# Turning an attention tile's weights two steps behind its scores instead of one

## The chip, the core and the metric

One core of a Trainium2 chip runs the whole program. The metric is the device time of one execution in microseconds; lower is better. Five engines work side by side, each in the order of its own queue: TensorE (PE; its weight loads are shown apart as PEld), VectorE (DVE), ScalarE (ACT), GpSimdE (POOL), and SyncE (SP), which here issues most DMAs. [...]

## The reference

Clustered attention on 2 batches of 8 heads (768 positions, 64 wide), then two mixture-of-experts layers on the 1536 rows of 512 that it gives. The part that matters here:

```python
q_assign = np.argmax(np.einsum('bhsd,hcd->bhsc', q_n, c_n), axis=-1)
k_assign = np.argmax(np.einsum('bhsd,hcd->bhsc', k_n, c_n), axis=-1)
mask = q_assign[:, :, :, None] == k_assign[:, :, None, :]
scores = scale * np.matmul(q, k.transpose(0, 1, 3, 2))
scores = np.where(mask, scores, -1000000000.0)
scores = scores - np.max(scores, axis=-1, keepdims=True)
attn = np.exp(scores)
attn = attn / (np.sum(attn, axis=-1, keepdims=True) + 1e-09)
return np.matmul(attn, v).astype(np.float32)
```

After it come `_moe_ref` (top 2 of 8 experts, noisy logits) and `_moe2_ref` (one expert for each row, with a capacity), each with weights of 512x1024 and 1024x512 for each expert.

## The kernel before

The attention goes through 16 heads of 6 tiles (128 queries by 768 keys): 96 steps `g`, and `LAG` more in which the pipeline runs empty. Float32 values are split into a high and a low part so that products run in a fast format. A step has four slots `s`, and its work is emitted in this order, which is each engine's order:

- Slots 0 and 1: `scores` for one half of the keys, two matmuls each (L678, L679), into the PSUM pool `pst` of two tiles. After slot 1, `top` takes the row maximum on VectorE (L684).
- Slots 2 and 3: `turned_part` turns one half of the tile before: three transposes (L703) into the PSUM pool `pet` (tiles named `et`, three buffers), a copy to `Eh` on ScalarE (L706), the remainder to `El` on VectorE (L707), which frees the `et` buffer.
- In each slot `go_av`: the matmuls of weights with values (`av`, L719 and L721) of a half of a head that is already turned, 12 for every 12 slots, spread as `AV` says (none in two slots, two in the last two). With the last of them ScalarE copies the result to `oT` (L724).
- In each slot `go`: what `PLAN` puts in this slot of the 24 of a head. CL0 to CL3 are the cluster products of the next head (L643) and start a chain of small VectorE steps, one for each later slot; QB, KA, QC and KB are transposes of q and k (L626), each into an `et` buffer with one copy on ScalarE (L629, L631, L633); XB is `xback` of the head before, which multiplies `oT` (L734) and scales (L730 to L742), adds to the logits on GpSimdE (L744) and, after odd heads, stores `xp` (L747); QS, KS and VS split q, k and v on GpSimdE.
- After slot 3, `weights`: the exponential of this step's tile (L692) on ScalarE, into the SBUF tile `E`, of which there are two.

From head 8 on the routing of the first batch (`route1`) runs in small pieces beside this, and in heads 12 to 15 the first experts' weights are split (`wneed0`; L180 on ScalarE, L182 on VectorE or GpSimdE). At the start of the last head `open_first` closes the pool `init`, which lies on the right side of SBUF, and opens the pools of the first expert there; the rows of that expert are turned in steps 2 and 4 of that head (L956, also `et` buffers). After the last step the pools of the attention are closed, and `ring3` with two more pairs of weight tiles lies where they were. The two expert layers follow, with no instruction in them that the change touches.

Of the kernel before, what the change touches and what calls it, by code (L numbers as in the profile page):

```python
# [8 lines left out]
F32 = mybir.dt.float32  # L9
F32R = mybir.dt.float32r  # L10
# [12 lines left out]
def kernel(  # L23
# [19 lines left out]
    C = centroids.shape[1]  # L43
    J = S // 128
    NBH = B * H
    HW = S // 2
    T, Dm = out.shape
    E, _, F = moe_w1.shape
    NT = T // 128
# [8 lines left out]
    NSP = 2  # L58
    NJ1 = E + 2
    GT = 3  # L60
# [7 lines left out]
    Z0, Z1, Z2 = (3, 0.5), (3, 0.5), (3, 2)  # L68
    NC1 = E * R1
    NC2 = (E + NSP) * CT2  # L70
    assert (B, H, S, D, C, E) == (2, 8, 768, 64, 16, 8) and cap % 128 == 0 and cap == 384

# [13 lines left out]
    consts = attn_ctx.enter_context(tc.tile_pool(name="aconst", bufs=1))  # L86
    init_ctx = ExitStack()
    init = init_ctx.enter_context(tc.tile_pool(name="init", bufs=1, side="right"))
# [10 lines left out]
    lane = glob.tile([128, 128], BF16, name="lane")  # L99
    first8 = glob.tile([128, E], F32, name="first8")  # L100
    eoff1 = glob.tile([128, E], F32, name="eoff1")
# [85 lines left out]
    def wfill():  # L187
        while clock["out"] < st.get("ahead", SB) and chunks and not st.get("rush"):
            clock["out"] += 1
            chunks.pop(0)()  # L190
# [16 lines left out]
    def advance(queue=tasks):  # L207
        for g in list(queue):
            try:
                next(g)  # L210
            except StopIteration:
                queue.remove(g)
# [299 lines left out]
    wk = attn_ctx.enter_context(tc.tile_pool(name="awork", bufs=2))  # L512
# [1 line left out]
    pet = attn_ctx.enter_context(tc.tile_pool(name="pet", bufs=3, space=PSUM))  # L514
    pav = attn_ctx.enter_context(tc.tile_pool(name="pav", bufs=1, space=PSUM))

    QTs = [consts.tile([128, J, 128 + C], F32R, name=f"qt{n}") for n in range(2)]
    KTs = [consts.tile([128, J, 192 + C], F32R, name=f"kt{n}") for n in range(2)]
    Vs = [consts.tile([128, J, 2, D], F32R, name=f"vt{n}") for n in range(2)]

    def load(i):
# [11 lines left out]
    def loadv(i):  # L533
        b, h = divmod(i, H)
        st["vraw", i] = io.tile([128, J, D], F32, name="vraw")
        nc.sync.dma_start(st["vraw", i], v[b, h].rearrange("(p j) d -> p j d", j=J))
# [134 lines left out]
    def scores(i, j, half):  # L671

        if half == 0:
            st["S", i, j] = pst.tile([128, 2, 512], F32, name="st")
        ps = st["S", i, j][:, half, :HW]
        js = slice(j * 128, (j + 1) * 128)
        cs = slice(half * HW, (half + 1) * HW)
        nc.tensor.matmul(ps, st["QC", i][:64 + C, js], st["KB", i][:64 + C, cs], start=True, stop=False)  # L678
        nc.tensor.matmul(ps, st["QB", i][:, js], st["KA", i][:, cs], start=False, stop=True)  # L679

    def top(i, j):
        ps = st["S", i, j][:, :, :HW]
        nm = wk.tile([128, 1], F32, name="nm", bufs=3)
        nc.vector.tensor_reduce(nm, ps, axis=AX.XY, op=OP.max, negate=True)  # L684
        st["nm", i, j] = nm

    def weights(i, j):

        if j == 0:
            st["Z", i] = wk.tile([128, J], F32, name="Z", bufs=3)  # L690
        E = wk.tile([128, 2, HW], F32, name="E", bufs=2)
        nc.scalar.activation(E, st.pop(("S", i, j))[:, :, :HW], AF.Exp, bias=st.pop(("nm", i, j)), accum_out=st["Z", i][:, j:j + 1])  # L692
        st["E", i, j] = E

    def turned_part(i, j, part):
        h, jj = divmod(j, 3)
        if jj == 0 and part == 0:
            st["W", i, h] = [wk.tile([128, J, HW], F32R, name=n) for n in ("Eh", "El")]
        Eh, El = st["W", i, h]
        E = st["E", i, j]  # L700
        ps = pet.tile([128, 512], F32, name="et")
        for n in range(3):
            nc.tensor.transpose(ps[:, n * 128:(n + 1) * 128], E[:, part, n * 128:(n + 1) * 128], ident)  # L703
        ps = ps[:, :HW].rearrange("p (n s) -> p n s", n=3)
        o = (slice(None), slice(3 * part, 3 * part + 3), slice(jj * 128, (jj + 1) * 128))
        nc.scalar.activation(Eh[o], ps, AF.Copy)  # L706
        nc.vector.tensor_sub(El[o], ps, Eh[o].bitcast(F32))  # L707
        if part:
            del st["E", i, j]

    def av(i, half, m):
        if m == 0:
            st["acc"] = pav.tile([128, 512], F32, name="acc")
        acc = st["acc"]
        Eh, El = st["W", i, half]
        t, low = divmod(m, 2)
        vt = Vs[i % 2][:, t]
        if low:
            nc.tensor.matmul(acc[:64, :HW], vt[:, 0], El[:, t], start=False, stop=(t == J - 1), skip_group_check=True)  # L719
        else:  # L720
            nc.tensor.matmul(acc[:, :HW], vt.rearrange("p a d -> p (a d)"), Eh[:, t], start=(t == 0), stop=(t == J - 1),  # L721
                             skip_group_check=True)
        if m == 2 * J - 1:
            nc.scalar.activation(oT[:, half * HW:(half + 1) * HW], acc[:, :HW], AF.Copy)  # L724
            del st["acc"], st["W", i, half]

    def xback(i):
# [17 lines left out]
        if h % 2 == 1:  # L745
# [2 lines left out]
                              [:, :, p * 128:(p + 1) * 128], xp.rearrange("p j a d -> p j (a d)"))  # L748


    LAG = 4
    RS = (1, 3, 5, 7, 9, 11, 13, 15, 17, 19, 21, 23)
    WS = {12: 10, 13: 10, 14: 22, 15: 0}
    AV = (0, 0, 1, 1, 1, 1, 1, 1, 1, 1, 2, 2)
    PLAN = {"CL0": 0, "CL1": 0, "CL2": 1, "CL3": 1, "QB0": 4, "QB1": 5, "KA0": 8, "KA1": 9, "QC0": 12, "KB0": 13,
            "XB": 17, "KB1": 16, "QC1": 20, "QS": 0, "KS": 2, "VS": 17}

    def plan(i):

        d = [[] for _ in range(24)]  # L760

        def put(name, fn, *args):
            d[PLAN[name]].append(lambda: fn(*args))

        if i + 1 < NBH:
            for n in range(4):
                put(f"CL{n}", cluster, i + 1, n)
            for n in range(2):
                put(f"QC{n}", trans, i + 1, "QC", n)
                put(f"KB{n}", trans, i + 1, "KB", n)  # L770
        if i + 2 < NBH:
            put("QS", splitq, i + 2)
            put("KS", splitk, i + 2)
            for n in range(2):
                put(f"QB{n}", trans, i + 2, "QB", n)
                put(f"KA{n}", trans, i + 2, "KA", n)
        if 1 <= i < NBH:
            put("XB", xback, i - 1)
        if i < NBH - 1:
            put("VS", vsplit, i + 1)  # L780
        return d
# [490 lines left out]
    def open_first():  # L1272
        init_ctx.close()
        P["first"] = (N2, pool("first", "ex", "right"), pool("first", "eh", "right"))
        st["pairs"] = True
        early_gather()
        st["preps"] = jobs[0].preps()
        st["first"] = jobs[0].hidden()

    for g in range(NBH * J + LAG):  # L1280
        i, t = divmod(g, J)
        if t == 0:
            steps = plan(i)
        if t == 2 and 1 <= i < NBH - 1:
            loadv(i + 1)
        if (i, t) == (3, 5):
            nc.sync.dma_start(out.rearrange("(p n) d -> p n d", n=NT),
                              xgs[0][:, None, :Dm].to_broadcast([128, NT, Dm]))
        if (i, t) == (5, 5):
            nc.sync.dma_start(y_dram.rearrange("(t p c) d -> p t c d", p=128, c=2)[:, :, 1],  # L1290
                              xgs[0][:, None, :Dm].to_broadcast([128, NT, Dm]))
        if (i, t) == (NBH - 6, 0):
            wfill()
        if i == H:
            steps[23] = steps[23] + [lambda: rtasks.append(route1(0, rpsum))] if t == 0 else steps[23]
        if (i, t) == (NBH - 1, 0):
            open_first()
        if (i, t) in PREP:
            st["preps"][PREP[i, t]]()
        if t == 0 and i in WS:  # L1300
            steps[WS[i]].append(wneed0)

        def go(s):
            for step in steps[s]:
                step()
            advance()
            if s in RS:
                advance(rtasks)

        def go_av(s):  # L1310

            w, k = divmod(4 * g + s - 16, 12)
            if 0 <= w < 2 * NBH:
                for m in range(sum(AV[:k]), sum(AV[:k + 1])):
                    av(*divmod(w, 2), m)

        ip, tp_ = divmod(g - 1, J)
        for s in range(4):
            if s < 2 and i < NBH:
                scores(i, t, s)  # L1320
                if s:
                    top(i, t)
            if s >= 2 and 0 <= ip < NBH:
                turned_part(ip, tp_, s - 2)
            go_av(s)
            go(4 * t + s)
            if s == 3 and i < NBH:
                weights(i, t)
# [278 lines left out]
```

## Time and profile before

| | us |
|---|---|
| median of 3 runs | 915.18 (913.13 to 916.36) |
| profiled execution | 916.56 |
| its span | 914.4 |
| TensorE busy, of the span | 855.0 |
| VectorE busy | 563.5 |
| ScalarE busy | 514.5 |
| GpSimdE busy | 225.8 |

The attention takes the first 320 us of the span. All times in the rows below are microseconds from the start of the span. A matmul's end is modelled and overlaps its successor's start, so the distance from start to start says what one costs.

### The profile page before, as it was taken

What the parts mean: (1) busy time and instruction counts of PE and PEld (TensorE: products, weight loads), DVE (VectorE), ACT (ScalarE), POOL (GpSimd) and SP (SyncE); (2) the same over time, 40 slices, a digit from 0 to 9 for tenths busy, and PEclk for the clock granted to TensorE, in tenths of its full rate; (3) what the DMA queues carried; (4) which work ended last, traced back from release to release, by engine and by line L of the source; (5) the groups of instructions that cost most, each with busy time, mean ns of one, the idle gap of its engine ahead of it and who ended that gap; (6) DMA issues with size and microseconds to landing.
All of it is one profiled execution on the core that took longest, in us unless ns stands there. A gap on an engine that the chain in (4) does not pass through costs nothing. (4 is left out here: it accounts for less than half of the span.)

```text
span 914.4 us, 14652 instructions
## 1 busy us (share of the span) xinstructions
PE 855.0 (94%) x5338; PEld 759.2 (83%) x5338; DVE 563.5 (62%) x1174; ACT 514.5 (56%) x977; POOL 225.8 (25%) x273
## 2 busy tenths in 40 slices
PE   5999999999999788899999999999998989999997
PEld 5899899888888677798897988888897768888886
DVE  5888888789898675544733535335375627655271
ACT  4888888888778632443433444336254427655361
POOL 4224223322222043023021230214223412222120
PEclk9999999999999999999999999999899989999999
DMA  3105331231111104555453454446464518776250
GB/s 78 43 27 190 105 121 44 73 116 44 51 50 39 51 18 154 164 177 166 150 190 127 129 162 150 139 155 213 152 227 159 189 34 270 253 231 196 76 175 16
DMA packets 61516, 116.73 MB, mean 128 GB/s; under 512 B 13065, under 2 KB 25097, under 8 KB 61424
## 3 DMA queue, kind: packets, MB, share of 16 engines
q1 hardware_dynamic: 52544, 92.50, 31.4%
q0 software_dynamic: 8880, 23.06, 7.5%
q8 instruction: 51, 0.84, 0.4%
q14 instruction: 41, 0.34, 0.1%
HBM read 97.24 MB, written 23.68 MB: 132 GB/s over the span
## 5 line engine op out<-in xcount | busy, mean ns | idle before, releaser
L182 DVE TENSOR_TENSOR wl<-raw,wh 128x1024 fp32r<-128x1024 f32 x120 | 145.3, 1222 | 41.1 <-ACT wh L180 37.0
L977 PE MATMUL l<-xh,wh 128*128 128x256 f32 (+1 forms) x508 | 157.6, 313 | 8.4 <-DVE hl L980 3.4
L977 PE MATMUL l<-xh,wl 128*128 128x256 f32 (+1 forms) x508 | 156.4, 310 | 0.2 <-DVE wl L182 0.2
L977 PE MATMUL l<-xl,wh 128*128 128x256 f32 (+1 forms) x508 | 150.2, 311 | 0.0
L1022 PE MATMUL l<-wh,hh 128*128 128x512 f32 x328 | 136.6, 416 | 0.8 <-PEq L1194 0.2
L180 ACT ACTIVATE wh<-raw 128x1024 fp32r<-128x1024 f32 x128 | 132.9, 1054 | 5.0 <-DMA raw<-in_moe_w_dram 4.9
L1024 PE MATMUL l<-wh,hl 128*128 128x512 f32 x328 | 131.3, 400 | 0.3 <-DVE hl L994 0.3
L1023 PE MATMUL l<-wl,hh 128*128 128x512 f32 x328 | 130.5, 398 | 0.0
L980 DVE SCALAR_TENSOR_TENSOR hl<-l,hh 128x256 fp32r<-128x256 f32 (+1 forms) x127 | 61.5, 484 | 103.6 <-ACT hh L979 101.5
L979 ACT ACTIVATE hh<-l 128x256 fp32r<-128x256 f32 (+1 forms) x127 | 54.9, 433 | 114.4 <-PE l L977 112.2
L707 DVE TENSOR_TENSOR El<-et,Eh 128x384 fp32r<-128x384 f32 x192 | 103.3, 554 | 21.2 <-ACT Eh L706 18.7
L703 PE MATMUL et<-ident,E 128*128 128x128 f32 x576 | 98.8, 282 | 15.2 <-ACT E L692 12.6
L706 ACT ACTIVATE Eh<-et 128x384 fp32r<-128x384 f32 x192 | 93.8, 491 | 27.3 <-PE et L703 24.7
L977 PEld LDWEIGHTS l<-xh,wh 128*128 128x128 f32 x508 | 96.9, 191 | 12.1 <-DVE hl L980 3.6
L684 DVE TENSOR_REDUCE nm<-st 128x1 f32<-128x768 f32 x96 | 91.6, 954 | 18.8 <-PE st L679 17.7
L977 PEld LDWEIGHTS l<-xh,wl 128*128 128x128 f32 x508 | 96.9, 191 | 1.2 <-DVE wl L182 0.4
L977 PEld LDWEIGHTS l<-xl,wh 128*128 128x128 f32 x508 | 95.3, 191 | 0.4
L703 PEld LDWEIGHTS et<-ident,E 128*128 128x128 f32 x576 | 68.4, 143 | 29.5 <-ACT E L692 23.2
L692 ACT ACTIVATE E<-st,nm 128x768 f32<-128x768 f32 x96 | 86.3, 899 | 2.7 <-DVE nm L684 2.7
L721 PE MATMUL acc<-Eh,vt 128*128 128x384 f32 x192 | 75.5, 393 | 0.6 <-ACT oT L724 0.6
L1024 PEld LDWEIGHTS l<-wh,hl 128*128 128x128 f32 x328 | 62.7, 191 | 15.5 <-DVE hl L994 0.8
L678 PE MATMUL st<-KB,QC 80*128 80x384 f32 x192 | 73.4, 383 | 0.1
(312 smaller groups left out, 1466.2 us busy)
## 6 DMA issues: line engine op xcount, KB each, us to landing
raw<-in_moe_w_dram SPq DMA_DIRECT2D x128, 512.0 KB, 4.4
vraw<-in_v_dram SPq DMA_DIRECT2D x16, 192.0 KB, 2.5
x_dram<-xp SPq DMA_DIRECT2D x8, 384.0 KB, 3.0
out_dram<-xg SPq DMA_DIRECT2D x1, 3072.0 KB, 12.1
y_dram<-xg SPq DMA_DIRECT2D x1, 3072.0 KB, 11.7
part<-y_dram SPq DMA_DIRECT2D x12, 256.0 KB, 4.1
yt<-y_dram SPq DMA_DIRECT2D x12, 256.0 KB, 4.6
x_dram<-part POOLq DMA_DIRECT2D x12, 256.0 KB, 3.9
```

Source lines behind the costliest of these rows:

```text
L180: nc.scalar.activation(wh[:, cs], raw[0], AF.Copy)
L182: eng.tensor_tensor(wl[:, cs], raw[0], wh[:, cs].bitcast(F32), op=OP.subtract)
L684: nc.vector.tensor_reduce(nm, ps, axis=AX.XY, op=OP.max, negate=True)
L692: nc.scalar.activation(E, st.pop(("S", i, j))[:, :, :HW], AF.Exp, bias=st.pop(("nm", i, j)), accum_out=st["Z", i][:, j:j + 1])
L703: nc.tensor.transpose(ps[:, n * 128:(n + 1) * 128], E[:, part, n * 128:(n + 1) * 128], ident)
L706: nc.scalar.activation(Eh[o], ps, AF.Copy)
L707: nc.vector.tensor_sub(El[o], ps, Eh[o].bitcast(F32))
L721: nc.tensor.matmul(acc[:, :HW], vt.rearrange("p a d -> p (a d)"), Eh[:, t], start=(t == 0), stop=(t == J - 1), skip_group_check=True)
L977: nc.tensor.matmul(ps[:, :n], (w1l if k == 2 else w1h)[:, c, fs], (self.xl if k == 1 else self.xh)[:, c, :n], start=(m == 0), stop=(m == l ...
L1022: nc.tensor.matmul(ps[:rows], hh[:, f, cs], w2h[:, f, :], start=(f == 0), stop=False)
L1023: nc.tensor.matmul(ps[:rows], hh[:, f, cs], w2l[:, f, :], start=False, stop=False)
L1024: nc.tensor.matmul(ps[:rows], hl[:, f, cs], w2h[:, f, :], start=False, stop=(f == FC - 1))
```

## The change

The transposes of a tile, and the value matmuls behind them, move one step back; the tile `E` gets a third buffer; the pipeline runs one step longer at its end; three entries of the plan move (XB from slot 17 to 21, QC1 from 20 to 17, VS from 17 to 20); and the split tiles of q and k (17 KB of each partition) move from the pool `aconst`, which lives as long as the attention, to `init`.

```diff
-    QTs = [consts.tile([128, J, 128 + C], F32R, name=f"qt{n}") for n in range(2)]
-    KTs = [consts.tile([128, J, 192 + C], F32R, name=f"kt{n}") for n in range(2)]
+    QTs = [init.tile([128, J, 128 + C], F32R, name=f"qt{n}") for n in range(2)]
+    KTs = [init.tile([128, J, 192 + C], F32R, name=f"kt{n}") for n in range(2)]
...
-        E = wk.tile([128, 2, HW], F32, name="E", bufs=2)
+        E = wk.tile([128, 2, HW], F32, name="E", bufs=3)
...
-    LAG = 4
+    LAG = 5
...
-            "XB": 17, "KB1": 16, "QC1": 20, "QS": 0, "KS": 2, "VS": 17}
+            "XB": 21, "KB1": 16, "QC1": 17, "QS": 0, "KS": 2, "VS": 20}
...
-            w, k = divmod(4 * g + s - 16, 12)
+            w, k = divmod(4 * g + s - 20, 12)
...
-        ip, tp_ = divmod(g - 1, J)
+        ip, tp_ = divmod(g - 2, J)
```

## Rows read from the trace of the kernel before

**Rows 1.** Busy time by engine, heads 1 to 8: from:to length, busy (instructions), clock, DMA.

```profile
36.00:183.00 147.00, 143.85 (x1092) 133.00 (x1091) 121.40 (x242) 126.13 (x290) 43.90 (x66) 1.00 0.28 92
```

**Rows 2.** Waits of TensorE, whole span: who for whom, us in total, times, longest.

```profile
PE et L703 <- ACT E L692: 12.6, 22, 2.0
```

**Rows 3.** The same wait from 36 to 183, 183 to 297, 297 to 320 us.

```profile
PE et L703 <- ACT E L692: 2.4, 8, 0.3
...
PE et L703 <- ACT E L692: 5.2, 8, 2.0
...
PE et L703 <- ACT E L692: 4.2, 4, 1.9
```

**Rows 4.** Time line, head 7's second step: start, us, instruction, [idle before]; last, head 8's first exponential.

```profile
145.85 0.91 ACT L692 ACTIVATE E<-st,nm 128x768 f32<-128x768 f32 x1
...
146.73 0.88 ACT L631 ACTIVATE QB<-et 128x384 fp32r<-128x384 f32 x2
...
146.90 0.55 PE L703 MATMUL et<-ident,E 128*128 128x128 f32 x3 [0.29 <-ACT E L692]
...
147.46 0.49 PE L703 MATMUL et<-ident,E 128*128 128x128 f32 x3
...
163.52 0.91 ACT L692 ACTIVATE E<-st,nm 128x768 f32<-128x768 f32 x1
```

**Rows 5.** Time line from the last value matmul of a half to xback.

```profile
153.24 0.34 PE L719 MATMUL acc<-El,vt 128*64 128x384 f32 x1
...
153.65 0.49 ACT L724 ACTIVATE oT<-acc 128x384 f32<-128x384 f32 x1
...
153.78 0.35 PE L626 MATMUL et<-identr,kt 128*80 128x128 f32 x3
...
154.19 1.48 PEld L734 LDWEIGHTS et<-RW,oT 128*128 128x128 f32 x12
```

**Rows 6.** Time line of the longest wait, head 9.

```profile
182.43 1.28 ACT L692 ACT_TABLE_LOAD   x1
...
184.62 0.86 ACT L631 ACTIVATE QB<-et 128x384 fp32r<-128x384 f32 x2
...
184.77 0.55 PE L703 MATMUL et<-ident,E 128*128 128x128 f32 x3 [2.02 <-ACT E L692]
```

**Rows 7.** Busy time by engine behind it; the granted clock is third from the end.

```profile
185.00:190.00 5.00, 5.00 (x29) 4.62 (x28) 2.96 (x9) 3.62 (x10) 0.00 (x0) 0.66 0.69 272
```

**Rows 8.** Time line, start of the last head: TensorE, VectorE, ScalarE.

```profile
296.28 0.55 PE L703 MATMUL et<-ident,E 128*128 128x128 f32 x3 [1.03 <-ACT E L692]
...
298.35 0.95 DVE L684 TENSOR_REDUCE nm<-st 128x1 f32<-128x768 f32 x1
299.21 1.01 DVE L707 TENSOR_TENSOR El<-et,Eh 128x384 fp32r<-128x384 f32 x2
299.39 0.90 ACT L692 ACTIVATE E<-st,nm 128x768 f32<-128x768 f32 x1 [0.98 <-DVE nm L684]
...
300.43 0.55 PE L703 MATMUL et<-ident,E 128*128 128x128 f32 x3 [1.87 <-ACT E L692]
```

**Rows 9.** Time line, the last tile's maximum and its transposes.

```profile
313.17 0.95 DVE L684 TENSOR_REDUCE nm<-st 128x1 f32<-128x768 f32 x1
...
315.25 0.55 PE L703 MATMUL et<-ident,E 128*128 128x128 f32 x3 [1.24 <-ACT E L692]
```

**Rows 10.** Time line, q's split on GpSimdE and the first transposes that read it.

```profile
159.24 1.02 POOL L574 TENSOR_TENSOR qt<-qraw,qt 128x384 fp32r<-128x384 f32 x1
...
163.28 0.37 PE L626 MATMUL et<-identr,qt 128*128 128x128 f32 x3
```

**Rows 11.** Time line behind the attention: the last store of xp, the second weight buffer's low half.

```profile
323.11 0.53 SPq L747 DMA_DIRECT2D x_dram<-xp  x1
...
327.19 4.86 POOL L182 TENSOR_TENSOR wl<-raw,wh 128x1024 fp32r<-128x1024 f32 x2 [3.40 <-ACT wh L180]
```

**Rows 12.** The page's DMA issues: stores of xp, KB each, median us to landing.

```profile
x_dram<-xp SPq DMA_DIRECT2D x8, 384.0 KB, 3.0
```

## What the change will do to the time

> **What bounds the kernel now.** I read the busy time by stage first. From 36 to 183 us, heads 1 to 8 of the attention, TensorE is busy 143.85 of 147.00 us at full granted clock, its weight loads 133.00, ScalarE 126.13 and VectorE 121.40 [rows 1]. The change touches nothing after the attention, so what it can win is TensorE's idle time inside the attention, and an end of the attention that comes earlier moves everything behind it by as much.
>
> Second I read TensorE's waits. The wait that the change aims at, the transposes at L703 for the exponentials at L692, is 12.6 us in 22 places [rows 2]. By stretch [rows 3]: 2.4 us in heads 1 to 8 (eight waits of 0.3, one for each head), 5.2 from 183 to 297 us (eight waits, one of 2.0), 4.2 in the last head (four); the 0.8 left over lie in the first head. So 12.6 us is the ceiling, 1.4% of the run, and two thirds of it lie in six single places.
>
> Third I read the time line around one wait of each kind, to see what else stands ready to stop TensorE there.
>
> **The new order.** Behind scores(t) TensorE now turns tile t-2, whose exponential ended a step ago. The weight-times-value matmuls follow at the same distance as before, so they stand one step (four slots) later too, and so does all that hangs on them: V's split (slot 17 to 20), the output product xback (17 to 21); QC1 goes from 20 to 17. TensorE's instructions are the same in number and kind. At the start tile 0 is turned one step later and at the end tile 95 is, one tile's six transposes and some value matmuls: work moved, not added. I take 0 for the start (0.8 us of waits there, bounds -0.8 to +0.8), since ScalarE's copies fill the first steps as much as TensorE's work.
>
> **Heads 1 to 8, the wait removed.** The eight waits of 0.29 go: the transposes that started at 146.90 could have at 146.61 [rows 4].
>
> **Heads 1 to 8, what is late next.** Two things. First, ScalarE's order is unchanged: exponential at 145.85, then the two QB copies from 146.73 [rows 4], 0.88 for both, so the first ends at about 147.2. The PSUM pool `et` has three buffers, and a step of four takes QB0, QB1 and the two halves of the turned tile: the second half takes QB0's buffer. It stands behind the exponential by that road, and the third E buffer doesn't touch it. Started with the first half at 146.61 and the value matmul between them (0.56 from half to half, 146.90 to 147.46), it would be ready at 147.17 and may go at about 147.27: a wait of 0.10, in the step with KA0 and KA1, which now has the two value matmuls. Bounds 0 and 0.29 (the whole wait over again).
>
> Second, xback loses its cover. Today the last value matmul of a half starts at 153.24, ScalarE copies it to oT from 153.65 to 154.14, and meanwhile TensorE does four score matmuls and KB1's three transposes; xback's first weight load, which reads oT, stands at 154.19 with no idle ahead of it [rows 5]. In the new plan KB1 (slot 16) lies ahead of the last value matmul (now slot 19), and between it and xback in slot 21 there are the four score matmuls alone. KB1 took from 153.78 to 153.96 and some 0.05 of the next start, so the load would be ready at about 153.95: a wait of 0.24. Bounds: 0, and 0.73 if the copy to oT also comes one more ScalarE copy later (0.49, the oT row), since KB1's and QC1's copies now lie in the same step ahead of it. I take 0.24: the step before xback now (two transposes, six value matmuls) has the make-up of today's (QC0, KB0, six), whose oT is ready as the row says.
>
> Sum of a head: -0.29 + 0.10 + 0.24 = +0.05; for eight +0.4. Bounds -2.4 (nothing late next) and 8 x (-0.29 + 0.10 + 0.73) = +4.3.
>
> [...]
>
> **Heads 9 to 14.** Six waits of 0.2 to 0.8 (5.2 less 2.0, and 1.0 that belongs to the end) make 2.2 us; the two new waits cost 6 x 0.34 = 2.0. Sum -0.2, bounds -2.2 and +2.8 (0.83 a head).
>
> **Head 9, 2.02 us.** At 182.43 ScalarE loads the exponential's table (1.28 us), and the exponential and QB's copies follow; TensorE stands until 184.77 [rows 6]. Now the first half of the turned tile can go at once, but the second needs QB0's copy, which ends at about 185.1, against 185.33 when it started before: 0.2 won, and some 0.15 more because oT's copy is no longer ahead of that exponential. I take -0.35, bounds 0 and -2.0. The granted clock of the five us after this stall was 0.66 [rows 7], a stretch at the lower of the two levels that cost about 0.34 x 5 = 1.7 us of work. Whether it comes again I can't read; 0, bounds -1.7 and +1.7 (one more such stretch).
>
> [...]
>
> **Head 15 and the end.** 1.03 and 1.87 us [rows 8] come from a chain on VectorE and ScalarE: a weight split holds the maximum back until 298.35, the exponential until 299.39. The change frees the turned tile from that exponential but the chain stays, and El, which frees an `et` buffer, is queued behind that maximum (from 299.21, the first ends at about 299.8). So the second half of the tile before could go at about 299.8 instead of 300.43, with the first half (0.3) done already: 0.9 of the 2.9 won. The other three (4.2 + 1.0 - 2.9, so 2.4 us) include 1.24 at 315.25, where the last tile's maximum at 313.17 stands behind xback's four VectorE operations and two El [rows 9]; the plan puts xback behind that maximum now. I take 0.7 of the 2.4, since El and the prepared rows of the first expert (in the same three buffers) are late next. Sum -1.6, bounds 0 and -5.3.
>
> **Edits at no cost.** V's split in GpSimdE's queue now precedes the sum into the logits and, as before, q's split: that split ended at 160.26 and is read at 163.28 [rows 10]; one and a half us of shift leave as much as cover. SyncE's store of xp moves one step and holds nothing that is due. With q's and k's tiles on the right, the later weight tiles lie over other attention tiles: the low half of the second weight buffer, by the sizes, over xp, whose store is issued at 323.11 and lands 3.0 us later at about 326.6, 0.5 us ahead of its first writer, on GpSimdE at 327.19 [rows 11, 12]. If that cover went, GpSimdE's writes would be late by as much; both move together.
>
> **The sum.** 0 + 0.4 - 0.2 - 0.35 - 1.6 = -1.75, about -1.7. The profiled execution took 916.56 us (span 914.4); this gives 914.9. It stood 1.4 above the median, 915.18, so the forecast for a median is 913.5.
>
> **Rivals.**
> 1. *Faster: nothing is late next.* For it: oT's copy and QB0's miss by only 0.2 and 0.1. Heads 1 to 14 give -2.4 - 2.2, head 9 -0.6, the end between -1.6 and -5.3: -6.8 to -10.5, so 905 to 908; with half of the new waits, about 911. Against it: the copy to oT can't start before its last matmul ends.
> 2. *Slower: ScalarE becomes the bound ahead of xback.* In the new plan four steps in a row hold two copies each. If the copy to oT is held by ScalarE's queue and not by its last matmul, it comes up to 0.49 later and xback waits 0.73: heads 1 to 8 +4.3, heads 9 to 14 +2.8, less 0.35 and 1.6, +5.1: 920.3. It decides from the point where ScalarE is idle nowhere between exponential and oT; for it, ScalarE's 126.13 of 147.00; against it, its idle in the steps of xback and of the clusters, where it catches up.
> 3. *It does what it says in name only:* each wait for L692 comes back as one for the copies behind it, to the full. 915.2.
>
> [...]
>
> **How the numbers follow.** A measurement of this kernel can tell about 0.3%, 2.75 us, from no change. Forecast 0.38, its own range 911.5 to 916.5; rival 3 0.08; rival 1 in whole or in half 0.36; rival 2, or a second stretch at the lower clock, 0.18. Forecast and rival 3 lie within 0.3%: 0.46. Faster 0.36, slower 0.18. Leaving out a tenth on either side gives 908.5 to 918.
>
> **What would show it.** Right: L703's waits for L692 under 2 us, new waits at L734 for L724 (about 0.2, once for each head), waits of L703 for copies, heads of 17.6 to 17.8 us (today 17.67, from 145.85 to 163.52 [rows 4]), the last head shorter by 1 to 2 us. Wrong: heads under 17.4 (rival 1), L734 waiting 0.5 or more (rival 2), a low clock somewhere new, or GpSimdE waiting at the second weight buffer.

## The result, and the profile after

The changed kernel takes 903.93 us, median of 4 runs (903.64 to 905.71); the kernel before, run beside it, 914.8 (913.13 to 916.36). The ratio is 0.9883, 95% interval 0.9858 to 0.9909: faster by 10.9 us. The forecast was 913.5, with a range down to 908.5: the sign of the gain was the forecast's, its size was not, and the time lies below the range. The profiled execution took 903.99.

First the page of the kernel after, part 1: the span, TensorE's busy time and its weight loads'.

```profile
span 902.2 us, 14571 instructions
PE 851.7 (94%) x5338; PEld 759.5 (84%) x5338; DVE 559.9 (62%) x1174; ACT 511.6 (57%) x977; POOL 224.5 (25%) x273
```

Next the place of the gain. I cut the span at the first score matmul, at the exponentials of the first tile of heads 1, 8 and 15, at the last value matmul and at the end. Busy time by engine in these five stretches: from:to length, busy (instructions) of PE, PEld, DVE, ACT, POOL, granted clock, share of the DMAs, GB/s. The kernel before:

```profile
17.96:39.79 21.83, 20.96 (x130) 18.93 (x130) 15.72 (x31) 15.79 (x37) 10.43 (x16) 1.00 0.15 43
39.79:163.52 123.73, 121.67 (x927) 112.76 (x925) 103.26 (x204) 106.38 (x246) 37.00 (x55) 1.00 0.28 93
163.52:299.39 135.87, 125.25 (x925) 112.87 (x923) 118.35 (x288) 112.04 (x250) 33.31 (x47) 0.99 0.21 65
299.39:319.46 20.07, 16.06 (x108) 13.89 (x109) 13.61 (x25) 13.25 (x28) 0.39 (x1) 1.00 0.10 32
...
319.46:914.40 594.94, 562.81 (x3206) 493.39 (x3204) 301.88 (x587) 257.66 (x399) 138.90 (x135) 0.98 0.48 157
```

The kernel after, the same cuts:

```profile
17.52:37.08 19.56, 19.26 (x115) 17.22 (x116) 14.04 (x27) 14.24 (x34) 10.43 (x16) 1.00 0.16 52
37.08:158.05 120.97, 120.96 (x926) 112.98 (x925) 101.70 (x204) 104.58 (x247) 36.90 (x55) 1.00 0.28 94
158.05:292.82 134.77, 125.39 (x934) 114.48 (x932) 118.69 (x290) 111.47 (x251) 32.97 (x48) 0.99 0.21 65
292.82:311.49 18.67, 16.52 (x112) 14.62 (x113) 14.35 (x27) 13.96 (x31) 0.39 (x1) 1.00 0.11 39
...
311.49:902.20 590.71, 561.26 (x3206) 492.80 (x3204) 300.58 (x587) 258.04 (x399) 138.12 (x135) 0.98 0.48 158
```

The attention went from 301.50 to 293.97 us (319.46 - 17.96, 311.49 - 17.52), so it gives 7.5: 2.3 in the first stretch, 2.8 in heads 1 to 7 (0.39 a head), 1.1 in heads 8 to 14, 1.4 in the last. The stage behind it, in which no instruction differs, is 4.2 shorter in these two profiles; the experiments come back to that. In heads 1 to 7 the stretch lost 2.76. The matmuls' idle time explains less of it, 2.05 (2.06 to 0.01); the weight loads' fell from 10.97 (123.73 - 112.76) to 7.99, by 3.0.

### The profile page after: what moved, and what is told of

Its sections match the earlier page's. It is cut to its first block, busy times and chain, and to the rows that moved or that the text cites. A ratio compares the mean times of both kernels' runs of the same rounds, so it can differ in the third digit from the quotient of the medians.

```text
span 902.2 us, 14571 instructions
## 1 busy us (share of the span) xinstructions
PE 851.7 (94%) x5338; PEld 759.5 (84%) x5338; DVE 559.9 (62%) x1174; ACT 511.6 (57%) x977; POOL 224.5 (25%) x273
## 5 line engine op out<-in xcount | busy, mean ns | idle before, releaser
L706 ACT ACTIVATE Eh<-et 128x384 fp32r<-128x384 f32 x192 | 91.2, 493 | 19.9 <-PE et L703 17.7
L684 DVE TENSOR_REDUCE nm<-st 128x1 f32<-128x768 f32 x96 | 91.4, 952 | 16.2 <-PE st L679 13.6
L1022 PEld LDWEIGHTS l<-wh,hh 128*128 128x128 f32 x328 | 63.0, 192 | 12.7 <-issue 1.0
```

What stands on the lines that cost most here:

```text
L1022: nc.tensor.matmul(ps[:rows], hh[:, f, cs], w2h[:, f, :], start=(f == 0), stop=False)
```

## The experiments

Medians; "before" is the kernel before, run beside it on the same chip. "Heads" is the mean length of heads 1 to 7, from exponential to exponential of the first tiles, "attention" and "behind" are the two stages as above, in the profiled execution.

| kernel | us | before | ratio (95%) | heads | attention | behind |
|---|---|---|---|---|---|---|
| before | | | | 17.68 | 301.5 | 594.9 |
| the change | 903.93 | 914.8 | 0.9883 (0.9858 to 0.9909) | 17.28 | 294.0 | 590.7 |
| the change again | 906.1 | 921.24 | 0.9858 (0.9817 to 0.9899) | 17.26 | 293.7 | 592.8 |
| memory alone | 915.91 | 914.29 | 1.0008 (0.9979 to 1.0037) | 17.68 | 302.9 | 596.2 |
| plan alone | 917.19 | 914.29 | 1.0042 (1.0017 to 1.0068) | 18.01 | 306.2 | 589.1 |
| order without memory | 905.72 | 914.29 | 0.9920 (0.9889 to 0.9952) | 17.27 | 294.3 | 593.8 |
| other order in xback | 902.0 | 914.29 | 0.9878 (0.9844 to 0.9913) | 17.44 | 294.7 | 591.5 |
| KA1 two slots later | 906.57 | 921.24 | 0.9860 (0.9824 to 0.9895) | 17.26 | 293.3 | 590.9 |
| QC1 back in slot 20 | 908.23 | 921.24 | 0.9873 (0.9840 to 0.9907) | 17.30 | 293.6 | 594.0 |
| KA1 and KB0 later | 910.9 | 921.24 | 0.9905 (0.9870 to 0.9940) | 17.28 | 295.7 | 592.4 |
| weight split later | 904.12 | 912.84 | 0.9898 (0.9857 to 0.9940) | 17.28 | 293.5 | 589.7 |
| xback in slot 20 | 901.63 | 912.84 | 0.9878 (0.9828 to 0.9928) | 17.33 | 293.8 | 587.4 |

Theory after the result: the gain is in the order of TensorE's work, the wait for the exponential was larger than the matmul rows said, and the wait that was forecast ahead of xback isn't there. Rivals: the third buffer or the new memory layout makes the gain; the plan makes it.

**Memory alone.** The kernel before, with the third `E` buffer and q's and k's tiles in `init`:

```diff
-    QTs = [consts.tile( ...
+    QTs = [init.tile( ...
-    KTs = [consts.tile( ...
+    KTs = [init.tile( ...
-        E = wk.tile([128, 2, HW], F32, name="E", bufs=2)
+        E = wk.tile([128, 2, HW], F32, name="E", bufs=3)
```

> The kernel before with the memory edits alone: q's and k's split tiles in the pool closed early, and three E tiles; the order of the work is as before. Theory (the gain comes from the order of the work): 915, within 1.5 us of before, with the weight loads of L703 still waiting about 23 us for L692. Rival (a part of the gain, the 4 us that the changed kernel won after 340 us, comes from where the tiles lie): 910 to 912, and the stage behind the attention shorter by 4.

Ratio 1.0008, heads as before. Waits of the weight loads, 36 to 183 us:

```profile
PEld et L703 <- ACT E L692: 6.3, 16, 0.4
```

They are those of the kernel before (6.4 in 16, below): neither a buffer nor the layout was short. The attention's 1.4 us more go with the granted clock: summed over 5 us windows, (1 - clock) x 5 is 3.4 in it, 1.7 in the kernel before. The gap repeats in each head (16 waits in eight heads) and the third buffer alone gave nothing; the row named the true cause, an exponential still running (0.91 us from 145.85, the transposes behind it at 146.90 [rows 4]).

**Plan alone.** The kernel before, with the three entries moved:

```diff
-            "XB": 17, "KB1": 16, "QC1": 20, "QS": 0, "KS": 2, "VS": 17}
+            "XB": 21, "KB1": 16, "QC1": 17, "QS": 0, "KS": 2, "VS": 20}
```

> The kernel before with the three entries of the plan alone (xback in slot 21, QC1 in 17, V's split in 20), the transposes one step behind as before. Theory (the distance of the transposes wins, not the plan): within 3 us of 915, heads 1 to 8 at 17.5 to 17.9 us. Rival (the plan evens out ScalarE's copies and is most of the gain): heads 1 to 8 at about 17.3 us and 908 or less.

Heads of 18.01, above the 17.5 to 17.9 expected: with the old distance the plan costs 0.33 a head. Its waits, 36 to 183 us, of the weight loads and of the matmuls:

```profile
PEld et L703 <- ACT E L692: 7.7, 16, 0.5
...
PE et L703 <- ACT E L692: 5.3, 16, 0.4
```

From here to the change the only step in the heads is the distance (the third buffer did nothing above). The weight loads' wait of 0.96 a head (7.7 / 8) goes, 0.25 comes (2.0 / 8, the wait for KA shown below), which makes -0.71; the matmuls' wait of 0.66 a head (5.3 / 8) goes and none comes. The heads went from 18.01 to 17.28, -0.73. In this step both measures are near what was won.

**Order without memory.** The change with two `E` buffers and q's and k's tiles back in `aconst`:

```diff
-    QTs = [init.tile( ...
+    QTs = [consts.tile( ...
-    KTs = [init.tile( ...
+    KTs = [consts.tile( ...
-        E = wk.tile([128, 2, HW], F32, name="E", bufs=3)
+        E = wk.tile([128, 2, HW], F32, name="E", bufs=2)
```

> The changed kernel with both memory edits undone: two E tiles, q's and k's split tiles where they were; the order of the work is that of the change. An exponential that writes a tile's E stands on ScalarE behind the copy of the transposes that read it last, so two tiles should do. Theory: 904, within 1.5 us of the changed kernel. Rival (the third buffer or the placement is needed): 907 to 912, with L692 waiting for L703, or the stage after 340 us as long as before.

Busy time by engine of the attention and of the stage behind it:

```profile
17.60:311.92 294.32, 282.49 (x2083) 260.01 (x2084) 248.80 (x545) 243.50 (x559) 80.64 (x119) 0.99 0.23 74
311.92:905.70 593.78, 563.82 (x3206) 494.89 (x3204) 300.35 (x587) 257.56 (x399) 139.27 (x135) 0.97 0.48 157
```

The attention is as short as the change's, 294.3. Two buffers do: the exponential that writes the buffer anew stands on ScalarE behind the copies to `Eh` of the transposes that read it last. In the change such a pair of copies starts at 142.51 and 143.15, and the exponential behind them at 143.91.

**Other order in xback.** The change, with the products that need the copy just made put first:

```diff
-        for j in range(J):
+        for j in (3, 4, 5, 0, 1, 2):
```

> The changed kernel with xback's six products in the order 3, 4, 5, 0, 1, 2, so that the first one reads the half of oT that was copied last. It tests the wait that my prediction priced at 0.24 us for each head and that the changed kernel does not show. Theory (the wait is not there because the first three products read the half copied long before): 0.2 to 0.3 us a head at L734, 15 heads, 907 to 909. Rival (oT comes early enough in any order): 904, no waits at L734.

The time line around xback, the change first (start, us, engine line instruction):

```profile
151.06 0.34 PE L719 MATMUL acc<-El,vt 128*64 128x384 f32 x1
...
151.47 0.48 ACT L724 ACTIVATE oT<-acc 128x384 f32<-128x384 f32 x1
...
151.77 0.81 PEld L734 LDWEIGHTS et<-RW,oT 128*128 128x128 f32 x6
```

And with the other order, with the wait's sum from 34 to 176 us:

```profile
151.22 0.48 ACT L724 ACTIVATE oT<-acc 128x384 f32<-128x384 f32 x1
...
151.75 0.97 PEld L734 LDWEIGHTS et<-RW,oT 128*128 128x128 f32 x8 [0.22 <-ACT oT L724]
...
PEld et L734 <- ACT oT L724: 1.8, 8, 0.2
```

In the change the load starts at 151.77 while the copy to `oT` runs until 151.95. Products 0 to 2 read the half that was copied 12 slots earlier; only products 3 to 5 need this one. Turned round, xback waits 0.22 in each head, almost the 0.24 of the prediction, and the heads grow by 0.16. The price was right; its place was wrong. The 907 to 909 expected of the whole run did not come: its median, 902.0, is not to be told from the change's.

**The change again.** Unchanged, beside the next three.

> The changed kernel once more, for a second profile on another day of clocks. Attention from the first score matmul to the last value matmul: 294.0 us, within 0.5, as in its first profile. The stage behind it was 590.7; before it was 594.9, and it lay between 589 and 596 in kernels that don't touch it. Theory (that part of the difference is the granted clock and no effect of the change): it comes out elsewhere in 589 to 596. Rival (the stage behind is shorter for good): 590.7 again, within 0.5.

The attention is the same within 0.3 us (293.7), the stage behind 2.1 longer, elsewhere in 589 to 596 as the theory had it.

**KA1 two slots later.** This is for the one wait that the change has left in a head.

```diff
-... "KA0": 8, "KA1": 9, ...
+... "KA0": 8, "KA1": 11, ...
```

> The changed kernel with KA1 in slot 11 instead of 9. The second half of the turned tile then no longer takes the PSUM buffer that KA0 filled in the same step, so it need not wait for KA0's copy behind the exponential. Theory: the eight waits of L703 for L633 (2.0 us by the weight loads in heads 1 to 8) go, heads 1 to 8 at 17.0 to 17.15 us instead of 17.28, 901 to 903. Rival (another buffer release, QC0 or KB0 for El, is late next): heads 17.25 to 17.4, time as the changed kernel.

Waits of the weight loads, 34 to 176 us:

```profile
PEld et L626 <- ACT KA L633: 1.9, 9, 0.4
PEld et L626 <- DVE El L707: 1.7, 7, 0.2
```

The wait moved from the turned tile to KA1 itself, 1.9 us for 2.0, and a second one came; the heads won 0.02 at most, as the rival said. The loads' waits rose from 2.0 to 3.6 us and the heads did not grow, so a wait of the loads is not always time lost. Here, with three `et` buffers and four users in a step, taking the wait from one user gave it to another.

**QC1 back in slot 20.** One of the three plan entries undone.

```diff
-... "QC1": 17, ...
+... "QC1": 20, ...
```

> The changed kernel with QC1 back in slot 20. It tells what that entry of the plan is worth. Theory (it spreads ScalarE's copies and is not where the gain is): heads 1 to 8 within 0.1 us of 17.28. Rival (two copies ahead of the exponential of step 4 cost or save): heads off by more than 0.15.

Heads of 17.30 and the same wait for KA (2.0 in 8): in the heads this entry is worth 0.02 at most.

**KA1 and KB0 later.**

```diff
-... "KA1": 9, "QC0": 12, "KB0": 13, ...
+... "KA1": 11, "QC0": 12, "KB0": 15, ...
```

> The changed kernel with KA1 in slot 11 and KB0 in slot 15. In heads 10 to 13 the routing takes an et buffer between KB0 and the first transposes of the turned tile, which then wait 1.1 us for QC0's copy, three times (2.9 us by the weight loads). Theory: these three waits go as well, 899 to 901. Rival (KB0 in slot 15 crowds KB1 and QC1 behind it, with waits for El instead): heads longer than 17.3 and no gain on KA1 alone.

The steady heads are as in the run with KA1 alone, but the attention is 2.4 longer than there: head 10 takes 18.23 (17.68 in the change), head 11 20.15 (19.65), where the routing also wants `et` buffers. The 899 to 901 expected did not come.

**Weight split later.** The split of the expert's weights that holds back a maximum at the start of the last head, two slots later:

```diff
-... 14: 22, 15: 0}
+... 14: 22, 15: 2}
```

> The changed kernel with the weight split of the last head moved from slot 0 to slot 2, behind the maximum of its first tile in VectorE's queue. In the changed kernel El of the tile before stands behind that maximum, which waits for the split, and the second half of the next turned tile waits 1.52 us for El. Theory: that wait goes, and the attention lasts 292.3 to 292.9 us instead of 293.9 (1.0 to 1.5 won); 902 to 904 in all. Rival (the split, 1.06 us on ScalarE and 1.23 on VectorE, is late wherever it stands): the wait comes back under L703 or L956 within the head, and the attention stays at 293.5 or more.

Waits of the matmuls, 289 to 312 us:

```profile
PE et L956 <- DVE El L707: 0.7, 1, 0.7
PE acc L721 <- ACT oT L724: 0.6, 1, 0.6
PE et L703 <- DVE lt L742: 0.5, 1, 0.5
PE et L703 <- DVE El L707: 0.4, 1, 0.4
```

The single wait of 1.5 us at the start of the last head (shown below) is gone, but L956 now waits 0.7 for an `El` that stands behind the same split on VectorE, and the attention, 293.5, is shorter by 0.2 to 0.4 than in the change's two profiles. So the 1.5 us came from VectorE's order there, and the rival was right: most of it comes back elsewhere.

**xback in slot 20.**

```diff
-... "XB": 21, ...
+... "XB": 20, ...
```

> The changed kernel with xback in slot 20, two score matmuls after the last value matmul instead of four. Its first product reads the half of oT that was copied twelve slots before; the fourth one, 0.74 us later, reads the half just copied. Theory: still no wait of L734 for L724, or under 0.1 us a head, and heads 1 to 8 within 0.15 us of 17.28. Rival (oT is waited for as a whole): 0.4 us at L734 in each head.

No wait for `oT` here either; the wait for KA shrinks to 0.5 and one for `El` of 1.7 takes its place. Heads 17.33, attention 293.8: no change. Heads 11 and 12, though, take 18.79 and 20.71 us where the change has 19.65 and 21.41, and the wait of the routing that is shown below is gone; the first stretch (20.1 after 19.6) and the last (19.7 after 18.7, at a mean granted clock of 0.91) are longer instead. 901.63 is the lowest median of all, but its stage behind, which it doesn't touch, makes it (587.4). Its interval and those of the change overlap widely, so no version tried here can be told from the change as faster.

**The stage behind the attention.** Twelve profiles have it unchanged, and it takes 587.4 to 596.2 us. Its length goes with the granted clock in the main. The lost time, (1 - clock) x 5 summed over 5 us windows, is 6.8 in the kernels with 587.4, 589.1 and 590.9, and 13.6, 11.9 and 15.4 in those with 594.9, 596.2 and 593.8 (not strictly: the change has 590.7 with 11.9). The kernel before, two such windows:

```profile
740.00:745.00 5.00, 1.88 (x5) 1.31 (x6) 0.00 (x0) 0.69 (x1) 1.66 (x2) 0.77 0.14 48
745.00:750.00 5.00, 5.00 (x14) 3.87 (x13) 0.00 (x0) 0.60 (x1) 2.37 (x3) 0.55 0.20 49
```

TensorE stood idle for 3.1 us of the first, and of the second all but the last half microsecond was granted 0.50 to 0.51. In windows of 0.5 us the two profiles, before and after, show a clock of 1.00 or 0.50 and nothing else but where one passes into the other (0.51 to 0.96); here it is 0.50 from 743.0 to 749.0. Of the 10.9 us between the medians, 7.5 are in the attention and about 3.4 here. The three profiles with the old distance have a mean of 593.4, the nine with the new one 591.5; with a scatter of some 2 to 4 us from run to run in either group these means are no proof.

In this one place, however, the kernels differ in every profile. The kernel before, the stop in it and the stretch around it, from one group of transposes at L991 to the second one behind it; last, the same stretch in the kernel after:

```profile
744.06 0.28 PEld L1001 LDWEIGHTS l<-wl,xh 128*128 128x128 f32 x1 [2.55 <-issue]
...
735.26:753.76 18.50, 15.38 (x61) 11.88 (x60) 2.96 (x6) 4.40 (x7) 4.03 (x4) 0.82 0.10 28
...
728.30:742.66 14.36, 12.87 (x62) 10.04 (x61) 3.34 (x6) 4.51 (x7) 4.03 (x4) 1.00 0.12 36
```

The three kernels with the old distance, the plan alone among them, have this stop (2.55, 2.89 and 2.65 us) and take 18.50, 18.21 and 17.57 us for the stretch; the nine with the new distance do not have it and take 14.29 to 14.37. So 3.2 to 4.2 us behind the attention go with the distance, and the nine ratios, 0.9858 to 0.9920 with a mean of 0.9884 (10.6 us of 914.8), show more than the attention's 7.5 in all but one. Why the stop comes with one order and not with the other stays open: "issue" says that the profile shows no wait for it, and the instructions are the same. Elsewhere the stage scatters both ways; a stop of 1.7 to 2.5 us at L1449 stands in five of the nine and in none of the three.

## Why the prediction was wrong, point by point

In the attention the prediction's sum was -1.75; -7.5 was measured. Term by term (heads 1 to 8 hold head 8 here too, 19.94 us after 20.2):

| term | predicted | bounds | measured |
|---|---|---|---|
| heads 1 to 8 | +0.4 | -2.4, +4.3 | -3.0 |
| heads 9 to 14 but for head 9's long wait | -0.2 | -2.2, +2.8 | +0.34 (heads 10 to 14) |
| head 9 | -0.35 | -2.0, 0 | -1.2 (19.21 to 18.03) |
| start and end | -1.6 | -6.1, +0.8 | -3.7 (2.3 + 1.4) |

**The wait was priced too low.** [rows 2] and [rows 3] gave 12.6 us in all and 2.4 in heads 1 to 8, from the matmuls. The weight loads of the same transposes waited almost twice that. The kernel before, waits of the weight loads, whole span and 36 to 183 us, and one head's two waits:

```profile
PEld et L703 <- ACT E L692: 23.2, 39, 2.2
...
PEld et L703 <- ACT E L692: 6.4, 16, 0.4
...
146.90 0.31 PEld L703 LDWEIGHTS et<-ident,E 128*128 128x128 f32 x3 [0.43 <-ACT E L692]
...
158.11 0.31 PEld L703 LDWEIGHTS et<-ident,E 128*128 128x128 f32 x3 [0.36 <-ACT E L692]
```

A head has two waits and not one, 0.79 us and not 0.29: the matmul at 146.90 shows 0.29 [rows 4] where its load shows 0.43, and the second wait, at 158.11, shows in no matmul row, since the matmul ahead (0.33 us from 157.79) is drawn as running until 158.12. Over the whole span the same waits are 23.2 by the loads and 12.6 by the matmuls. This is the first failed step: the term of -0.29 a head was taken as the most that the heads could give, and they gave 0.39 although the wait for KA came. The loads' waits are no exact price either: 0.79 less KA's 0.25 makes 0.54, and 0.39 was measured; with products turned round in xback 0.22 more of them cost 0.16. The truth lay between the two rows.

**xback's wait was put where it isn't.** The prediction let xback wait for the whole of `oT`, at 0.24 a head. Its first three products read the older half, so no wait came; with the order turned round it came at 0.22. This second failed step is worth 1.9 us in heads 1 to 8 and 1.4 of the 2.0 laid on heads 9 to 14.

**The wait for KA's copy was right.** It was put at 0.10 a head (bounds 0 and 0.29), in the step with KA0 and KA1, in the buffer that the first copy empties. The kernel after, the two steps:

```profile
141.64 0.98 ACT L631 ACTIVATE QB<-et 128x384 fp32r<-128x384 f32 x2
...
141.88 0.31 PEld L703 LDWEIGHTS et<-ident,E 128*128 128x128 f32 x3
...
143.91 0.91 ACT L692 ACTIVATE E<-st,nm 128x768 f32<-128x768 f32 x1
...
144.78 0.88 ACT L633 ACTIVATE KA<-et 128x384 fp32r<-128x384 f32 x2
...
145.33 0.31 PEld L703 LDWEIGHTS et<-ident,E 128*128 128x128 f32 x3 [0.26 <-ACT KA L633]
...
PEld et L703 <- ACT KA L633: 2.0, 8, 0.3
```

With QB the turned tile goes on without a wait; with KA the weight loads of its second half stand 0.26 for the first copy that follows the exponential. Place and mechanism are the prediction's. The size is 0.25 a head by the loads; the matmuls' rows show no wait there.

**What the plan costs.** With the old distance the three entries cost 0.33 a head. It is the same wait grown longer: by the loads from 6.4 to 7.7 in eight heads, 0.16 a head, and by the matmuls from 2.4 [rows 3] to 5.3, 0.36 a head, since now both waits of a head stand in their rows. With the new distance this wait is gone. What the whole plan costs there no run shows; QC1's entry is worth 0.02, and xback in slot 20 instead of 21 adds 0.04.

**Head 9.** The wait for QB's copy came as forecast (0.85 by the matmul), and the granted clock of 180 to 185 us is 0.72, the dip of [rows 7] over again, so it gave nothing back. The kernel after:

```profile
176.69 1.28 ACT L692 ACT_TABLE_LOAD   x1
...
177.99 0.90 ACT L692 ACTIVATE E<-st,nm 128x768 f32<-128x768 f32 x1
...
178.88 0.86 ACT L631 ACTIVATE QB<-et 128x384 fp32r<-128x384 f32 x2
...
179.41 0.90 PE L703 MATMUL et<-ident,E 128*128 128x128 f32 x3 [0.85 <-ACT QB L631]
...
180.00:185.00 5.00, 5.00 (x31) 4.60 (x30) 3.71 (x10) 4.35 (x10) 0.00 (x0) 0.72 0.88 344
```

Of the 1.2 us some 0.4 is what each head won; the rest is the long wait made shorter, 2.02 [rows 6], now 0.85 and 0.27 ahead of it. The exponential starts 1.30 us after the table load of 1.28 began, against 1.29 before (183.72 after 182.43). The dip does not always fall here: with KA1 two slots later it is between 250 and 260 us (0.77 and 0.89 in two windows of 5 us), with xback in slot 20 between 290 and 300 (0.88 and 0.78), and with the other order in xback the mean clock of the attention is 1.00. In the order without memory head 9 takes 16.93 us, and head 12 22.39 where the change has 21.41. So I estimate that about 1 us of a single profile's head can be the granted clock's.

**Heads 10 to 14 gave nothing.** Not for xback's wait, as forecast, but for the routing: two of its matmuls (L364) now wait for `lt`, the last read of xback's `et` buffer, one in head 11 and one in head 12, which L364 did nowhere before. The kernel after, waits of the matmuls and the longer of the two:

```profile
PE et L364 <- DVE lt L742: 2.3, 2, 1.1
...
250.28 0.25 DVE L742 TENSOR_TENSOR lt<-et,z 128x96 f32<-128x96 f32 x1
...
250.67 0.40 PE L364 MATMUL et<-ohv,ohp 128*128 128x96 f32 x2 [1.13 <-DVE lt L742]
```

With xback moved to slot 21 its buffer comes free later, and in these heads something else asks for it. Heads 11 and 12 are 0.3 and 0.6 longer than before. With xback in slot 20 L364 waits nowhere for `lt` and the two heads are 0.9 and 0.7 shorter than in the change, which bears this out. The prediction named the buffer pool, but only for heads without routing; that its -0.2 came near the sum is luck.

**Start and end.** The first stretch won 2.3, the last 1.4. Most of the first is work moved: the value matmuls start a step later (TensorE busy 20.96 to 19.26). At the end that work comes back, and yet the stretch shrank, because its idle time fell from 4.01 to 2.15 (20.07 - 16.06, 18.67 - 16.52). The mechanism forecast, `El` queued behind the maximum, is there. The kernel after:

```profile
291.77 0.95 DVE L684 TENSOR_REDUCE nm<-st 128x1 f32<-128x768 f32 x1
292.64 1.01 DVE L707 TENSOR_TENSOR El<-et,Eh 128x384 fp32r<-128x384 f32 x2
292.82 0.90 ACT L692 ACTIVATE E<-st,nm 128x768 f32<-128x768 f32 x1 [1.46 <-DVE nm L684]
293.24 0.55 PE L703 MATMUL et<-ident,E 128*128 128x128 f32 x3 [1.52 <-DVE El L707]
...
305.92 0.52 PE L703 MATMUL et<-ident,E 128*128 128x128 f32 x3 [0.55 <-DVE lt L742]
```

1.52 stands for the 1.03 and 1.87 of [rows 8], and 0.55 for the 1.24 of [rows 9]. By the matmuls' rows the start's 0.8 of waits went whole, where 0 had been taken, and the last stretch's 4.2 [rows 3] became 2.6 (1.52, 0.55 and one of 0.56): 2.4 of the 3.7. About 1.0 more is work that the cuts now put on the other side: the weight loads' busy time of the two stretches together went from 32.82 to 31.84, that of heads 8 to 14 from 112.87 to 114.48. So heads 10 to 14 did a little better, and start and end a little worse, than the table has it. The bounds held; the value taken was too careful. (The prediction's 4.2 + 1.0 - 2.9 is 2.3 and not 2.4, which changes nothing here.)

**The stage behind the attention was put at nothing.** The prediction held that all there is to win lies inside the attention. That is the third failed step: some 3.4 of the 10.9 us came behind it, where a stop of TensorE (2.55 to 2.89 us by the loads) is in each kernel with the old distance and in none with the new one. The granted clock of the stretch around it was 0.82 in the kernel before and 1.00 in the kernel after. The cause of the stop is not shown.

**Edits at no cost** were that: no engine waits for V's or q's split in the heads. q's split, from 155.24 to 156.25, still ends well before the next head's transposes, and the second weight buffer's writer, at 319.23, waits for ScalarE as in [rows 11], the store of xp having been issued at 315.16.

**The rivals.** The first, nothing late next, came nearest: 905 to 908 where 903.9 was measured, with a chance of 0.36; it too was counted from the matmuls' 12.6. Its -6.8 to -10.5 hold the attention's -7.5, yet something was late next, KA's copy, so a part of that is luck. The second fell: L734 waits nowhere in the change. The third fell too: of 0.79 us a head, by the loads, only 0.25 came back. The signs named in advance told them apart at once: heads of 17.28, under the 17.4 given for rival 1.

## What to carry to other kernels

For TensorE, read a wait in the weight loads' rows beside the matmuls': here 0.79 us a head against 0.29. Neither is the price. The matmuls' rows hid a whole wait, so they are no ceiling, and the heads gave 0.39. Before pricing a new wait, look at which part of the tile the first waiting instruction reads; half a tile copied long ago was the whole cover that the prediction missed. When one change moves distance, buffers and plan together, price and try each alone: in each head the buffers were worth nothing, the plan alone cost 0.33 and the distance then gave 0.73.

## What the runs showed of the hardware that I had not expected

A stage that nobody touched took 587.4 to 596.2 us in single profiles, 1.5% apart, in the main with the granted clock, so a gain of one per cent is better read from the length of its own stage, which repeated within 0.3 us (293.97 and 293.74), than from the whole. Yet it has to be looked at, stretch by stretch: a stop that the profile puts down to no wait was there in three profiles with the old order and absent from nine with the new one, and was worth 3.2 to 4.2 us. And a weight load may begin while the matmul ahead of it is still drawn as running: in the kernel before, a load of L679 starts at 145.89, and L678's matmul ahead of it is drawn from 145.82 to 146.23. There, 16 waits of the loads in eight heads left only 8 in the matmuls' rows.
